# Weight loads of the first two expert rounds wait for a GpSimd write made after the token gather

## The chip, the cores and the metric

The kernel runs on one core of a Trainium2 chip. The metric is the device time of one execution, in microseconds. Its engines are named as the profile names them: PE is TensorE, DVE is VectorE, ACT is ScalarE, POOL is GpSimd, SP is SyncE.

## The reference

A block of masked attention over 8 batches and 8 heads (576 positions, 64 channels a head) feeds a mixture of experts. The output of attention is 4608 tokens of 512 numbers. Routing is done by all pairs of token and expert in order of their score, with a capacity of 576 tokens for each of the 8 experts:

```python
logits = x @ w_gate
order = np.argsort(-logits.flatten())
for idx in order:
    tok, e = (int(idx) // E, int(idx) % E)
    if assigned[tok] >= 0 or counts[e] >= cap:
        continue
    assigned[tok] = e
    counts[e] += 1
for e in range(E):
    mask = assigned == e
    h = np.maximum(x[mask] @ w1[e], 0.0)
    out[mask] = h @ w2[e]
```

All is in float32; w1 is 512x1024 and w2 is 1024x512 for each expert.

## The kernel before, in words

The first third of the time is attention; it writes its result, the tokens x, to a buffer `xd` in device memory. The rest is `moe`, in eight rounds, one for each expert in the order in which experts fill up. Round r finds out which expert is next (`search`), which tokens it takes (`settle`, `listing`), fetches those tokens (`gather`), and runs two products on them (`expert`). The search and the listing of round r+1 lie between the products of round r.

- `gather` fetches 576 tokens by five indirect DMAs that GpSimd issues (four of 128 tokens, one of 64) into `xg`. PE transposes each of them into a PSUM tile (`ptx`, a single buffer from round 1 on; in round 0 `py` too), ACT makes `xh` and DVE makes `xl` from it, so that x = xh + xl in two parts that PE can multiply fast. In round 0 PE also runs filler products on a tile of zeros between the transposes (`keep_clock`).
- `weights` brings one of the 8 tiles of w1 or of w2 (f = 0 to 7, 128x512, 256 KB): SP issues the load into a `raw` buffer (8 for w1, 4 for w2), ACT makes the high part, and the low part comes in one of two ways. Mostly DVE subtracts. For w2 of round 0 and for w1 and w2 of round 1 (`ADDED`), ACT writes the negated high part and GpSimd issues a DMA that adds `raw` to it: an accumulating transfer.
- `expert` runs the first product (`ph`, from `xh`, `xl` and the w1 parts, f = 0 to 7), ACT and DVE bring the result to `hb`, and the second product (`py`, from `hb` and the w2 parts). ACT and DVE bring that to `y`, and GpSimd issues an indirect DMA that scatters it to `out` behind a one-element write (`spacer`).

There are two kinds of DMA queue: SP's loads go through q1, all that GpSimd issues (gathers, scatters, accumulating transfers) through q0. Both run on the same 16 DMA engines.

The order of the instructions on each engine is made by a planner when the program is built (`Schedule`): every step is given an engine, an estimated cost, its dependencies and a boost, and the planner writes the instructions of each engine in the order that its estimates give. The order is fixed; what waits for what on the chip is settled from the buffers that instructions share. A dependency that a step is given in the planner alone moves its place in the order and makes no instruction wait. So it is with `behind` before the change: from tile f = 3 on, the loads of round 0 are planned after the second gather (`got[r, 1]`), and on the chip SP issues them without a wait.

```python
RAW1, D_R, NQ, AHEAD_W = 8, 262, (2, 2), (3,)
def behind(r, f):
    return [got[r, 1]] if r < len(AHEAD_W) and f >= AHEAD_W[r] else []
ld = op("SP", 60, load, [*deps, *old], dma=T_W)
```

Of the kernel before, what the change touches and what calls it, by code (L numbers as in the profile page):

```python
# [36 lines left out]
TOL_DVE, TOL_ACT, TOL_POOL, TOL_PE, T_W = 100, -50, 200, 500, 730  # L37
T_P, T_S, AHEAD = 440, 2150, 5
B_L, B_G, B_T, B_X, B_H, B_HL, B_Y, B_S, B_W = 23000, 27000, 15000, 0, 20000, 17000, 28000, -15000, 1500
RAW1, D_R, NQ, AHEAD_W = 8, 262, (2, 2), (3,)  # L40
ADDED, T_A, T_G = (("2", 0), ("1", 1), ("2", 1)), 4500, 4500
NS, B_E, DIRECT = (2, 2), 3000, 6
B_C = (0, 2500, 20000, 20000, 20000, 20000, 20000, 20000)
# [112 lines left out]
class Schedule:  # L156
# [8 lines left out]
    def op(self, eng, cost, fn, deps=(), boost=0, lat=0, dma=0, buf=None):  # L165
        x = Op(len(self.ops), eng, cost, fn, deps, boost, lat, dma, buf)
        for d in x.deps:
            d.users.append(x)
        self.ops.append(x)
        return x  # L170
# [926 lines left out]
def moe(tc, ctx, C, R, xd, w1, w2, out):  # L1097
    nc = tc.nc
# [4 lines left out]
    NF, ND = FF // 128, DM // 128  # L1103
    CUT = (0, 256, CAP)
    K = Schedule({"DVE": TOL_DVE, "ACT": TOL_ACT, "POOL": TOL_POOL, "PE": TOL_PE})
    op = K.op
# [19 lines left out]

    act = lambda o, i, f=AF.Copy: nc.scalar.activation(o, i, f)  # L1127
    sub = lambda e, o, a, b: e.tensor_tensor(o, a, b, op=OP.subtract)  # L1128
    E, gemm1_end, x_users, got = {}, {}, {}, {}

    def weights(n, r, f, deps):

        raw, old, use = RAW[n].take()

        def load():
            if n == "1":
                src = w1[bass.ds(E[r], 1), f].rearrange("o p d f -> p (o d f)")
            else:
                src = w2[bass.ds(E[r], 1), f * 128:f * 128 + 128, :].rearrange("o p d -> p (o d)")
            nc.sync.dma_start(raw, src)  # L1140

        ld = op("SP", 60, load, [*deps, *old], dma=T_W)
        h, oldh, useh = WH[n].take()
        l, oldl, usel = WL[n].take()
        hi = op("ACT", 525, lambda: act(h, raw), [ld, *oldh], B_W)
        if (n, r) in ADDED:
            use.append(hi)
            ne = op("ACT", 525, lambda: nc.scalar.activation(l, h.bitcast(F32), AF.Copy, scale=-1.0), [hi, *oldl], B_W)
            useh.append(ne)
            lo = op("POOL", 1040, lambda: nc.gpsimd.dma_start(l, raw, accum_op=OP.add), [ne], B_W, lat=T_A)  # L1150
            use.append(lo)
        else:
            lo = op("DVE", 600, lambda: sub(nc.vector, l, raw, h), [ld, hi, *oldl], B_W)
            use += [hi, lo]
        useh.append(lo)
        return h, l, hi, lo, useh, usel


    def chain(eng, cost, fn, deps, boost=None):
        return op(eng, cost, fn, deps, B_C[len(scan)] if boost is None else boost)  # L1160
# [3 lines left out]
    def search(r):  # L1164
        scan.append(r)
        prev = st["next"]
        hold = gemm1_end.get(r - AHEAD)
        g = prev + [hold]
        for v in range(2):
            for it in range(4):  # L1170
                p = chain("PE", T_P, R.counts, g)

                def dve(v=v, it=it):
                    R.step(it, v)
                    if it == 3 and v == 0:
                        R.low()
                        R.flags(R.V2, None, R.kstep(0, True))

                g = [chain("DVE", T_S + (400 if it == 3 and not v else -1050 if it == 3 else 0), dve, [p])]

        def which():
            R.count()
            R.fills()
            R.expert(R.largest())
            R.above()

        return chain("DVE", 2100, which, [g[0], st["fetch"]])

    def settle(r, e):

        if r < NE - 1:
            m = chain("DVE", 1180, R.members, [e], B_L)
            rk = chain("PE", 70, R.ranks, [m], B_L)
            nd = st["need"] = chain("DVE", 310, R.need_of, [m, st.get("slots")], B_L)
        else:
            nd = chain("DVE", 400, R.rest, [e, st["left"], st["slots"]], B_L)
            rk = chain("PE", 70, R.ranks, [nd], B_L)
        ac = chain("DVE", 1000, R.accept, [rk, nd], B_L)
        sl = st["slots"] = chain("DVE", 450, R.slots, [ac, st.get("digits")], B_L)
        ix, box = listing(r, sl)  # L1200
        st["left"] = None
        if r == NE - 2:
            st["left"] = chain("DVE", 200, R.assign, [ac])
        elif r < NE - 1:
            cl = chain("DVE", 1780, R.close, [nd, ix if r == 0 else None])
            lv = chain("DVE", 880, R.leave, [cl, ac])
            oc = chain("ACT", 1055, lambda: R.copies(R.oh, nc.scalar), [lv])
            gf = chain("DVE", 670, R.start, [cl])
            st["next"] = [oc, gf]
        return ix, box  # L1210
# [21 lines left out]
    def gather(r, ix, box):  # L1232

        done = []
        for m, n in enumerate(MSZ):
            xg, old, use = XG.take()

            def get(xg=xg, n=n, m=m):
                nc.gpsimd.indirect_dma_start(out=xg[:n], out_offset=None, in_=xd,  # L1239
                                             in_offset=bass.IndirectOffsetOnAxis(ap=box[0][:n, m:m + 1], axis=0))  # L1240

            g = op("POOL", 1040, get, [ix, *old], B_G, lat=T_G if r else 2600)
            got[r, m] = g
            if r == 0:
                pt, old, usep = (PYR if m % 3 < 2 else PTR).take()
            else:
                pt, old, usep = PTR.take()
            pt = pt.rearrange("p (d x) -> p d x", d=ND)
            a, b = (x[:, :, 128 * m:128 * m + n] for x in (XH, XL))

            def turn(pt=pt, xg=xg, n=n):
                for d in range(ND):
                    nc.tensor.transpose(pt[:, d, :n], xg[:n, 128 * d:128 * d + 128], C["identf"][:n, :n])  # L1253

            t = op("PE", 460 if n == 128 else 250, turn, [g, *old], B_T)
            use.append(t)
            if r == 0:
                turns.append(t)
            full = 500 if n == 128 else 290
            wx = x_users.get((r - 1, 0 if m < 2 else 1), [])  # L1260
            s0 = op("ACT", full, lambda pt=pt, a=a, n=n: act(a, pt[:, :, :n]), [t, *wx], B_T)
            s1 = op("DVE", full + 100, lambda pt=pt, a=a, b=b, n=n: sub(nc.vector, b, pt[:, :, :n], a), [s0], B_T)
            usep += [s0, s1]
            done.append((s0, s1))
        return done
# [6 lines left out]

    def expert(r, X, box, W1, W2):

# [47 lines left out]
        for m, n in sorted(enumerate(MSZ), key=lambda x: x[1] if r == NE - 1 else 0):  # L1322
            py, old, use = PYR.take()
            for f in range(NF):
                hb, _, useb, hl = hidden[f]
                wh, wl, hi, lo, useh, usel = W2[f]

# [39 lines left out]
    def fetch(r, eidx):  # L1367
        E[r] = nc.values_load(eidx[0:1, 0:1], engines=[nc.sync.engine], min_val=0, max_val=NE - 1,
                              skip_runtime_bounds_check_because="the index is the place of a maximum among NE flags")

    X, BOX, W, EN = {}, {}, {}, {}

    def round_(r):
        e = None
        if r:
            e = search(r) if r < NE - 1 else chain("DVE", 650, R.last, [st["fetch"], st["need"]])
        en = st["fetch"] = EN[r] = op("SP", 100, lambda: fetch(r, R.eidx), [e])
        ix, BOX[r] = settle(r, e)
        X[r] = gather(r, ix, BOX[r])
        W[r] = [weights("1", r, f, [en, *behind(r, f)]) for f in range(NF)]  # L1380

    def behind(r, f):

        return [got[r, 1]] if r < len(AHEAD_W) and f >= AHEAD_W[r] else []

    round_(0)
    for r in range(NE):
        W2 = [weights("2", r, f, [EN[r], *behind(r, NF)]) for f in range(NF)]
        expert(r, X[r], BOX[r], W[r], W2)
        if r + 1 < NE:  # L1390
            round_(r + 1)
# [51 lines left out]
def build(tc, T, out):  # L1443
    with ExitStack() as ctx:
        cp = ctx.enter_context(tc.tile_pool(name="const", bufs=1))
        dp = ctx.enter_context(tc.tile_pool(name="scratch", bufs=1, space=DRAM))
        C, load_const = load_consts(tc, cp, T)
        xd = dp.tile([N, DM], F32, name="xd")
        Lt = cp.tile([128, NCH, NE], F32, name="Lt")
        R = Router(tc, ctx, C, Lt)  # L1450
        with ExitStack() as c2:
            attention(tc, c2, C, load_const, T, xd, Lt, R)
        with ExitStack() as c2:
            moe(tc, c2, C, R, xd, T["in_moe_w1"], T["in_moe_w2"], out)
# [15 lines left out]
```

## Time and profile before

| | |
|---|---|
| median of 3 runs | 720.18 us (719.6 to 720.63) |
| profiled execution | 720.37 us |
| its span, first to last instruction | 718.6 us |
| PE busy | 678.6 us, 94% of the span |
| DVE busy | 484.2 us, 67% |
| ACT busy | 291.1 us, 41% |
| POOL busy | 137.3 us, 19% |
| moved by DMA | 104.62 MB |

Times in the rows are microseconds from the start of the span. An instruction's row names what it writes and reads without the buffers' numbers; an idle stretch ahead of it is given with what ended it. Busy time of an engine leaves out register moves, semaphores and SP's DMA issues. The granted clock is a share of PE's full speed: 1.00 is 2.4 GHz, 0.50 is 1.2 GHz. A DMA queue's row gives packets, MB and the share of the 16 engines' time that its packets took in the stretch.

### The profile page before, as it was taken

What the parts mean: (1) busy time and instruction counts of PE and PEld (TensorE: products, weight loads), DVE (VectorE), ACT (ScalarE), POOL (GpSimd) and SP (SyncE); (2) the same over time, 40 slices, a digit from 0 to 9 for tenths busy, and PEclk for the clock granted to TensorE, in tenths of its full rate; (3) what the DMA queues carried; (4) which work ended last, traced back from release to release, by engine and by line L of the source; (5) the groups of instructions that cost most, each with busy time, mean ns of one, the idle gap of its engine ahead of it and who ended that gap; (6) DMA issues with size and microseconds to landing.
All of it is one profiled execution on the core that took longest, in us unless ns stands there. A gap on an engine that the chain in (4) does not pass through costs nothing.

```text
span 718.6 us, 17416 instructions
## 1 busy us (share of the span) xinstructions
PE 678.6 (94%) x6598; PEld 596.5 (83%) x6598; DVE 484.2 (67%) x2081; ACT 291.1 (41%) x617; POOL 137.3 (19%) x204
## 2 busy tenths in 40 slices
PE   7899999999984799799999999999999999999995
PEld 5788889998973598589889879788978978988984
DVE  5578877698237689579679868868978963823300
ACT  3355454543310383575334423514533434423310
POOL 6111111100000332741410310311221031221011
PEclk9999999999975799999999999999999999999998
DMA  9999999972111674978223513511532383122001
GB/s 249 260 269 294 264 301 267 281 198 55 47 35 36 207 147 106 292 172 238 96 67 118 169 63 92 200 45 52 167 135 67 118 291 130 56 74 97 1 22 45
DMA packets 58525, 104.62 MB, mean 146 GB/s; under 512 B 6212, under 2 KB 27844, under 8 KB 58436
## 3 DMA queue, kind: packets, MB, share of 16 engines
q1 hardware_dynamic: 49096, 78.32, 38.0%
q0 software_dynamic: 9344, 25.17, 12.8%
q8 instruction: 52, 0.85, 0.5%
q14 instruction: 33, 0.27, 0.1%
HBM read 78.31 MB, written 18.87 MB: 135 GB/s over the span
## 4 chain that ended last, share of the span: by engine, by line
PE 74%; issue 11%; DVE 6%; DMA 4%; POOL 3%; ACT 1%; POOLq 0%; SPq 0%; DVEq 0%
PE ph L1290 24%; PE py L1332 15%; PE pS L506 9%; PE px L514 6%; PE px L564 3%; PE pS L503 3%; DMA xg<-xd,idx 2%; PE pm L486 2%; PE pz L768 2%; PE ptx L1253 2%; PE px L654 2%; PE py L1335 1%; PE py L1337 1%; POOL out L1358 1%; DMA qs<-in_qd 1%
## 5 line engine op out<-in xcount | busy, mean ns | idle before, releaser
L1332 PE MATMUL py<-w2h,hb 128*128 128x512 f32 x512 | 173.6, 403 | 1.4 <-ACT w2h L1127 1.3
L1290 PE MATMUL ph<-xh,w1h 128*128 128x256 f32 (+1 forms) x512 | 138.7, 301 | 0.0
L1290 PE MATMUL ph<-xl,w1h 128*128 128x256 f32 (+1 forms) x512 | 136.2, 297 | 0.0
L1290 PE MATMUL ph<-xh,w1l 128*128 128x256 f32 (+1 forms) x512 | 136.0, 296 | 0.0
L1332 PEld LDWEIGHTS py<-w2h,hb 128*128 128x128 f32 x512 | 97.3, 190 | 21.8 <-ACT w2h L1127 2.3
L1332 PE MATMUL py<-w2l,hb 128*128 128x512 f32 x256 | 101.3, 396 | 0.8 <-DVE w2l L1128 0.5
L1127 ACT ACTIVATE hb<-ph 128x256 fp32r<-128x256 f32 (+2 forms) x192 | 59.7, 346 | 103.1 <-PE ph L1290 102.3
L1290 PEld LDWEIGHTS ph<-xh,w1h 128*128 128x128 f32 x512 | 91.5, 190 | 0.4
L1290 PEld LDWEIGHTS ph<-xh,w1l 128*128 128x128 f32 x512 | 91.6, 190 | 0.0
L1290 PEld LDWEIGHTS ph<-xl,w1h 128*128 128x128 f32 x512 | 91.5, 190 | 0.0
L506 PE MATMUL pS<-q,k 128*80 128x96 f32 (+1 forms) x672 | 84.2, 267 | 0.0
L1358 POOL DMA_INDIRECT out<-y,idx x40 | 40.1, 1003 | 205.9 <-ACT y L1127 145.0
L456 ACT ACTIVATE E<-pS 96x384 f32<-96x384 f32 (+1 forms) x96 | 46.7, 486 | 71.5 <-PE pS L506 70.4
L1310 DVE SCALAR_TENSOR_TENSOR hb<-ph,hb 128x320 fp32r<-128x320 f32 (+1 forms) x128 | 57.4, 453 | 26.5 <-ACT hb L1127 22.5
L506 PEld LDWEIGHTS pS<-q,k 128*80 128x80 f32 (+1 forms) x672 | 69.7, 161 | 0.1
L1127 ACT ACTIVATE y<-py 128x512 f32<-128x512 f32 (+1 forms) x40 | 23.9, 596 | 104.9 <-PE py L1332 90.1
L493 DVE CUSTOM_DVE_ANT_0 junkm<-pm,const 128x80 bf16<-128x80 f32 (+1 forms) x336 | 59.4, 243 | 5.1 <-PE pm L486 4.5
L1332 PEld LDWEIGHTS py<-w2l,hb 128*128 128x128 f32 x256 | 48.8, 191 | 10.6 <-DVE w2l L1128 1.1
L514 PE MATMUL px<-v,E 81*64 81x65 f32 (+1 forms) x1344 | 47.7, 225 | 2.9 <-ACT E L456 2.4
L1127 ACT ACTIVATE w1h<-raw 128x512 fp32r<-128x512 f32 x64 | 38.5, 628 | 29.3 <-DVE oa L1060 22.0
L1239 POOL DMA_INDIRECT xg<-xd,idx x40 | 40.2, 1005 | 50.1 <-PE ph L1290 31.1
L1128 DVE TENSOR_TENSOR w2l<-raw,w2h 128x512 fp32r<-128x512 f32 x48 | 31.7, 685 | 26.4 <-ACT w2h L1127 22.9
(168 smaller groups left out, 1036.5 us busy)
## 6 DMA issues: line engine op xcount, KB each, us to landing
raw<-in_moe_w SPq DMA_DIRECT2D x128, 256.0 KB, 3.7
v<-in_vp SPq DMA_DIRECT2D x8, 780.0 KB
v<-in_vd SPq DMA_DIRECT2D x8, 650.0 KB
xd<-xs SPq DMA_DIRECT2D x16, 288.0 KB, 8.9
xd<-xs SPq DMA_DIRECT2D x32, 144.0 KB, 10.0
w2l<-raw POOLq DMA_DIRECT2D x16, 256.0 KB
qs<-in_qp SPq DMA_DIRECT2D x7, 576.0 KB, 8.6
k<-in_kp SPq DMA_DIRECT2D x7, 576.0 KB, 10.4
```

What stands on the lines that cost most here:

```text
L456: e = self.op("ACT", 380, lambda j=j, pS=pS: nc.scalar.activation(self.E[:self.nk, j * self.gs:j * self.gs + self.gs], pS.tile[:, :self.gs ...
L493: nc.vector.tensor_tensor_reduce(out=jk[:, c - c0, :nk], in0=pm[:, (c - c0) * nk:(c - c0 + 1) * nk], in1=mm[:, min(1, (c if self.kind == 0 ...
L503: nc.tensor.matmul(pS[:nk, c - c0], ls[:64 + n, c], self.r[:64 + n, :2 * nq], start=(c == c0), stop=False, skip_group_check=True)
L506: nc.tensor.matmul(pS[:nk, c - c0], self.Ks[c], self.Qm[c], start=False, stop=True, skip_group_check=True)
L514: nc.tensor.matmul(px[64 * a:64 * a + 64, c - c0], lh, self.V[c][a], start=True, stop=True)
L1127: act = lambda o, i, f=AF.Copy: nc.scalar.activation(o, i, f)
L1128: sub = lambda e, o, a, b: e.tensor_tensor(o, a, b, op=OP.subtract)
L1239: nc.gpsimd.indirect_dma_start(out=xg[:n], out_offset=None, in_=xd, in_offset=bass.IndirectOffsetOnAxis(ap=box[0][:n, m:m + 1], axis=0))
L1290: nc.tensor.matmul(o, a[:, d * 128:d * 128 + 128], b[:, d, c0:c1], start=((d, i) == pairs[0]), stop=((d, i) == pairs[-1]))
L1310: hl = op("DVE", 335 if j == 0 else 400, lambda: nc.vector.scalar_tensor_tensor(hb[:, CAP + c0:CAP + c1], o, 0.0, hb[:, c0:c1], op0=OP.max ...
L1332: nc.tensor.matmul(py, x, w, start=(f + i == 0), stop=(f == NF - 1 and i == 2))
L1358: s = nc.gpsimd.indirect_dma_start(out=out, out_offset=bass.IndirectOffsetOnAxis(ap=box[0][:n, m:m + 1], axis=0), in_=y[:n], in_offset=None)
```

## The change

`behind` goes. In its place, when the tile f = `AHEAD_W[r]` of w1 of round r is planned, GpSimd gets a step that writes one zero into the `raw` buffer of that tile, planned after the second gather and after the last users of the buffer. The load writes the same buffer, so on the chip it waits for the write. The steps of all later tiles of that round, of w1 and w2, depend on it in the planner, and on SP they stand behind the waiting load. `AHEAD_W` goes from (3,) to (3, 4): in round 0 three tiles of w1 are loaded ahead of the write, in round 1 four.

```diff
-RAW1, D_R, NQ, AHEAD_W = 8, 262, (2, 2), (3,)
+RAW1, D_R, NQ, AHEAD_W = 8, 262, (2, 2), (3, 4)
...
-    E, gemm1_end, x_users, got = {}, {}, {}, {}
+    E, gemm1_end, x_users, got, gate = {}, {}, {}, {}, {}
 
     def weights(n, r, f, deps):
 
         raw, old, use = RAW[n].take()
+        if n == "1" and r < len(AHEAD_W) and f == AHEAD_W[r]:
+
+            gate[r] = op("POOL", 100, lambda: nc.gpsimd.memset(raw[:1, :1], 0.0), [got[r, 1], *old], B_G)
+        if r in gate:
+            deps = [*deps, gate[r]]
...
-        W[r] = [weights("1", r, f, [en, *behind(r, f)]) for f in range(NF)]
-
-    def behind(r, f):
-
-        return [got[r, 1]] if r < len(AHEAD_W) and f >= AHEAD_W[r] else []
+        W[r] = [weights("1", r, f, [en]) for f in range(NF)]
...
-        W2 = [weights("2", r, f, [EN[r], *behind(r, NF)]) for f in range(NF)]
+        W2 = [weights("2", r, f, [EN[r]]) for f in range(NF)]
```

The order of PE, of DVE and of SP is the same in both programs, row for row. What moves stands on GpSimd and ACT, and SP gets two waits.

SP, the loads of round 0, now (`raw10` to `raw17` are the buffers of w1, `raw20` to `raw23` those of w2; the rows between are register moves):

```order
L1145 DMA raw11_3213<-in_moe_w1 128x512
L1145 ISA
L1145 DMA raw12_3214<-in_moe_w1 128x512
L1145 ISA
L1145 DMA raw13_3215<-in_moe_w1 128x512 [waits Pool_49]
L1145 ISA
L1145 DMA raw14_3216<-in_moe_w1 128x512
L1145 ISA
L1145 DMA raw20_3220<-in_moe_w2 128x512
```

The fourth load, of `raw13`, now waits for GpSimd, and the rest stand behind it; before, none of these rows had a wait for GpSimd. In round 1 the fifth, of `raw14`, has it. On GpSimd in round 0 the write stands right behind the fifth gather.

GpSimd at the gathers of round 1, before:

```order
L1239 DMA xg4_3260<-xd_66,idx_4375 64x512
L1150 DMA w1l3_3243<-raw13_3215 128x512
L1150 DMA w1l4_3244<-raw14_3216 128x512
L1150 DMA w1l5_3245<-raw15_3217 128x512
L1150 DMA w1l6_3246<-raw16_3218 128x512
L1150 DMA w1l7_3247<-raw17_3219 128x512
L1357 MEMSET spacer_3204 1x1
L1358 DMA out_0<-y2_3274,idx_3642 4608x512
```

and now:

```order
L1244 DMA xg4_3260<-xd_66,idx_4367 64x512
L1155 DMA w1l3_3243<-raw13_3215 128x512
L1136 MEMSET raw14_3216 1x1
L1362 MEMSET spacer_3204 1x1
L1363 DMA out_0<-y2_3274,idx_3642 4608x512
L1362 MEMSET spacer_3204 1x1
L1363 DMA out_0<-y0_3272,idx_3642 4608x512
L1155 DMA w1l4_3244<-raw14_3216 128x512
L1155 DMA w1l5_3245<-raw15_3217 128x512
```

The write stands behind the five gathers and the accumulating transfer of tile 3; those of tiles 4 to 7 move behind two scatters and later.

ACT around the x copies of round 1, before:

```order
L1127 ACTIVATE w1h4_3228<-raw14_3216 128x512
L1148 ACTIVATE w1l4_3244<-w1h4_3228 128x512
L1127 ACTIVATE w1h5_3229<-raw15_3217 128x512
L892 ACTIVATE ohr_4399<-oh_4388 128x1152
L1148 ACTIVATE w1l5_3245<-w1h5_3229 128x512
L1127 ACTIVATE w1h6_3230<-raw16_3218 128x512
L1148 ACTIVATE w1l6_3246<-w1h6_3230 128x512
L1127 ACTIVATE y2_3274<-py0_3209 128x512
L1127 ACTIVATE w1h7_3231<-raw17_3219 128x512
L1148 ACTIVATE w1l7_3247<-w1h7_3231 128x512
L1127 ACTIVATE xh_3261<-ptx0_3211 128x4x128 x2
L1127 ACTIVATE y0_3272<-py1_3210 128x512
```

and now:

```order
L892 ACTIVATE ohr_4389<-oh_4379 128x1152
L1127 ACTIVATE y2_3274<-py0_3209 128x512
L1127 ACTIVATE xh_3261<-ptx0_3211 128x4x128 x2
L1127 ACTIVATE w1h4_3228<-raw14_3216 128x512
L1127 ACTIVATE y0_3272<-py1_3210 128x512
L1127 ACTIVATE xh_3261<-ptx0_3211 128x4x128
L1153 ACTIVATE w1l4_3244<-w1h4_3228 128x512
L1127 ACTIVATE w1h5_3229<-raw15_3217 128x512
L1153 ACTIVATE w1l5_3245<-w1h5_3229 128x512
L1127 ACTIVATE w2h0_3232<-raw20_3220 128x512
L1153 ACTIVATE w2l0_3248<-w2h0_3232 128x512
L1127 ACTIVATE xh_3261<-ptx0_3211 128x4x128
```

Tiles 4 to 7 of w1 move behind the first two x copies, and tile 4 now stands ahead of the copy of `y0` and of the third x copy.

## Rows read from the trace of the kernel before

**Rows 1.** The page: busy us (share of the span) xinstructions.

```profile
PE 678.6 (94%) x6598; PEld 596.5 (83%) x6598; DVE 484.2 (67%) x2081; ACT 291.1 (41%) x617; POOL 137.3 (19%) x204
```

**Rows 2.** PE's waits in 228:246, 246:410, 315:719: us, times, longest.

```profile
PE py L1253 <- DMA xg<-xd,idx: 2.8, 1, 2.8
...
PE ptx L1253 <- DMA xg<-xd,idx: 4.3, 1, 4.3
...
PE py L1332 <- ACT w2h L1127: 1.3, 1, 1.3
```

**Rows 3.** GpSimd's timeline: start, us, instruction, idle time before.

```profile
237.85 1.45 POOL L1239 DMA_INDIRECT xg<-xd,idx  x1 [3.35 <-DVE idx L1092]
...
243.38 0.91 POOL L1239 DMA_INDIRECT xg<-xd,idx  x1 [0.30 <-issue]
254.10 0.99 POOL L1150 DMA_DIRECT2D w2l<-raw  x1 [9.81 <-ACT w2l L1148]
...
285.93 0.87 POOL L1150 DMA_DIRECT2D w1l<-raw  x1
...
288.56 0.85 POOL L1150 DMA_DIRECT2D w1l<-raw  x1 [0.33 <-ACT w1l L1148]
...
291.06 1.03 POOL L1239 DMA_INDIRECT xg<-xd,idx  x1 [0.30 <-DVE A L1039]
...
297.43 0.97 POOL L1150 DMA_DIRECT2D w1l<-raw  x1 [0.34 <-issue]
...
304.60 0.09 POOL L1357 MEMSET spacer<- 1x1 f32 x1
...
342.58 1.08 POOL L1239 DMA_INDIRECT xg<-xd,idx  x1 [7.13 <-issue]
```

**Rows 4.** SP's timeline, 230:236.4: first start, us from first to last end.

```profile
230.19 6.27 SPq L1140 DMA_DIRECT2D raw<-in_moe_w  x12
```

**Rows 5.** DMA queues in 239:240 and in 240:241: packets, MB, share.

```profile
q1 hardware_dynamic: 208, 0.39, 100.3%
...
q0 software_dynamic: 24, 0.10, 24.6%
```

**Rows 6.** The chain in 220:360, round 0: start, us, what.

```profile
237.85 5.78 DMA xg<-xd,idx
...
249.30 3.98 PE ph L1290 x28
```

**Rows 7.** Stretches: us, busy (x) of each engine, PEclk, DMA share, GB/s.

```profile
243.25:243.50 0.25, 0.00 (x0) 0.00 (x0) 0.00 (x0) 0.00 (x0) 0.12 (x1) 0.50 0.65 229
302.00:304.00 2.00, 2.00 (x7) 1.62 (x6) 1.57 (x7) 0.26 (x1) 1.55 (x4) 0.50 1.11 209
```

**Rows 8.** DMA queues in 290:296.5.

```profile
q0 software_dynamic: 425, 0.81, 65.8%
q1 hardware_dynamic: 522, 0.95, 43.4%
```

**Rows 9.** The same chain, round 1.

```profile
291.06 9.71 DMA xg<-xd,idx
...
302.07 2.70 PE py L1332 x6
...
305.21 2.07 PE py L1332 x9
```

**Rows 10.** DMA queues in 344:345.5 (round 2).

```profile
q0 software_dynamic: 73, 0.25, 57.2%
```

**Rows 11.** DMA queues in 255.5:258.5 (two accumulating transfers of round 0).

```profile
q0 software_dynamic: 267, 0.51, 100.7%
```

**Rows 12.** A stretch with one search step on DVE (columns as in rows 7).

```profile
302.90:305.35 2.45, 2.45 (x11) 1.92 (x10) 2.21 (x11) 0.11 (x1) 1.51 (x4) 0.65 1.12 201
```

**Rows 13.** The tile raw in 225:345; and the page's DMA issues (last: median us).

```profile
DMA to landing us min/median/max: 3.0/4.9/5.5
...
raw<-in_moe_w SPq DMA_DIRECT2D x128, 256.0 KB, 3.7
```

## The prediction, made before the changed kernel ran

> **What bounds the kernel now.** I read the page first, then TensorE's waits, the timelines of GpSimd and SyncE, the DMA queues stretch by stretch, the chain of waits and the granted clock. TensorE is busy for 678.6 us, 94% of the span [rows 1]. The reader is to see that it sets the end: from 315 us on its longest wait is 1.3 us, so whatever an earlier stage gives or loses arrives at the end unchanged. Two of its waits are for the token gather: 2.8 us in expert round 0 and 4.25 us in round 1 [rows 2]. In these two rounds the change holds weight loads back.
>
> Round 0: GpSimd issues the five gathers from 237.85 to 244.29 [rows 3]. SyncE has by then posted twelve weight loads of 256 KB, from 230.19 on [rows 4]. In the microsecond from 239 they hold all of the DMA engines (100.3%); the gathers' queue q0 gets 24.6% in the next [rows 5]. The first transposes start 5.8 us after the first issue, and the dense products at 249.30 [rows 6]. In that wait the granted clock falls to 0.50, the lower of its two levels (1.2 GHz) [rows 7].
>
> Round 1: in GpSimd's order [rows 3] and so on q0 the gathers stand behind three accumulating transfers and a scatter. From 290 to 296.5 q0 moves 0.81 MB, about the three (0.79 MB), while the weight loads on q1 move 0.95 MB beside them [rows 8]. The first transposes come 9.71 us after the first issue [rows 9], and again the clock is at 0.50 afterwards [rows 7].
>
> **The change part by part.** PE, DVE and SP keep their order; GpSimd gets two one-element writes, and ACT and GpSimd take four weight tiles of round 1 later. The writes themselves cost nothing: the spacer write of the same size takes 0.09 us, and after the gathers of round 0 GpSimd has no work until 254.10 [rows 3]. What counts is what they hold: the gated load and everything behind it on SP, where only weight loads stand.
>
> *Round 0.* Three loads (0.79 MB) go out at once and are through by about 235; the other nine go out from about 244.6, when the gathers have been issued. So the gathers have the engines to themselves. The nearest row is round 2, where no weight load runs: the first gather, issued from 342.58 [rows 3], moves 0.25 MB between 344 and 345.5 [rows 10], and is through 2.9 us after its issue began. Here the first issue takes 0.37 us longer (1.45 against 1.08), so the data would be through at 241.1; landing needs a little more. Ends: 241.1 (2.6 us gained) and 243.67 (nothing). I take 241.9, near the uncontended row: **1.8 us**. At the lower clock transposes and filler take about 1.5 us a gather, slower than the 1.25 us between GpSimd's issues, so the whole chain up to 249.30 moves by that; at the full clock it would gain some 0.4 more. The late weights are covered: nine tiles, 2.36 MB, at the 0.39 MB a microsecond of the hardware queue alone [rows 5] are in by about 252, the first of them near 248.3, and its product is wanted some 9 us behind the first dense one, at about 256.
>
> *Round 1.* Four loads (1.05 MB) go out ahead of the gate and are through by about 287. The three accumulating transfers, issued from 285.93 on and the last from 288.56 [rows 3], then run alone. Two such transfers moved 0.51 MB in the 3 us from 255.5 [rows 11], 1.5 us each: they would be through at 291.7 instead of 296.5, the scatter at 292.6, the first gather, whose issue ends at 292.10, at about 294, landed by 295. TensorE wants it at 296.56. So the wait of 4.25 us goes, and with it the fallen clock: after the wait six products take 2.70 us, a moment later nine take 2.07 [rows 9]; 1.32 us lost there and 0.53 on transposes and counts, 1.85 in all. What is late next is the single buffer of the transposes. ScalarE and VectorE must empty it, VectorE in turn with a search step of 2.45 us [rows 12]; counted through, the third, fourth and fifth transposes would wait 0.3, 0.2 and 0.35 us, of which 0.15 is there already: 0.7 to be taken off. **4.25 + 1.85 - 0.7 = 5.4 us**. Ends: 0 (the transfers in front stay as slow) and 6.1.
>
> The price of the gate there: the write stands behind the fourth accumulating transfer, issued from 297.43 [rows 3], so the fifth load goes out at about 298.8. Loads take 3.0 to 5.5 us to land in this stretch, 3.7 in the median of all [rows 13]: 301.8 to 304.3, I take 302.5. ScalarE now has that tile ahead of a y copy and of the third x copy, which it would finish at 304.2; VectorE, after its search step, can start on that copy at 304.1. So it is just hidden; at 304.3 it would cost 1.8 us. The last w2 tile would be ready near 328 and is wanted after 335.
>
> **One rule against it.** The Trainium skill (DMA: Bandwidth & Descriptors, section Queues, rings and completion order) says that each DMA engine takes turns between the queues that have work, a packet at a time. By that rule the first gather of round 0 has its half of the engines already, and the sum there would be 0.7 us instead of 1.8. The rows from 239 to 241 do not agree with it [rows 5]; those from 290 to 296.5, with 65.8% and 43.4%, come near it [rows 8].
>
> **The sum.** 1.8 + 5.4 = 7.2 us off the profiled execution's 720.37 is 713.2. The median of the runs shown is 0.2 below that execution, so **713.0**.
>
> **Rivals.** (1) *Even turns.* In round 0 the gather has its share already and waits mostly for something fixed; emptying q1 saves half of the 1.4 us that its data takes alone, 0.7: 720.2 - 0.7 - 5.4, about 714.1. For it: both queues move in round 1. Against it: q0 has a quarter of the engines in the microsecond from 240, two issues on. (2) *The accumulating transfers are the brake by themselves.* They keep most of their 6.5 us without q1, the first gather lands near 299.5, and round 1 gives 1.3 us with the low clock still there: 720.2 - 1.8 - 1.3, about 717.0. Against it: 1.5 us each [rows 11]. (3) *Slower: ScalarE stands, in order, before the fifth tile of round 1.* From 302.5 on each microsecond that this tile lands later keeps the y copy, the third x copy and then TensorE waiting by as much. It decides from 309.7 on (302.5 + 7.2), 10.9 us after the issue; at 313 the time would be 723.5. Against it: no landing in this stretch took over 5.5 us [rows 13]. (4) *The hold holds nothing*, the loads being through before it acts or the gathers not bound by them: 720.2. Against it: twelve loads are posted before the first gather [rows 3, 4].
>
> **How the numbers follow.** Forecast 0.67, (1) 0.14, (2) 0.11, (4) 0.04, (3) 0.04. About 0.2% (1.4 us) is what can be told from no change here. Forecast, (1) and (2) are faster by more, less a hundredth for weak mixtures: 0.91; within 0.2%: 0.05; slower: 0.04. The low end takes both upper ends (2.6 + 6.1 = 8.7 us, 711.5) and half a microsecond of spread between runs: 711.0. The high end takes in (1), (2), and a fifth tile that costs its 1.8 us: 717.0.
>
> **What would show it.** Right: TensorE's two waits for the gather shrink, to about 1 us near 241 and to none near 296; q1 is empty from about 235 to 245 and from 287 to 299; no stretch at clock 0.50 around 300; the first transposes of round 1 start some 5.5 us after the gather's first issue instead of 9.71. Wrong: ScalarE's wait for the gated tile of round 1 is over 2 us and TensorE waits for x copies; or q0 still takes over 2 us for each accumulating transfer with q1 empty; or in round 0 the dense products start as long after the gather's first issue as before.

## The result, and the profile after

The changed kernel took 717.01 us in the median of 18 runs (713.69 to 722.36 but for one run that was disturbed), the kernel before 720.44 beside it. The ratio is 0.9939 with a 95% interval of 0.9916 to 0.9962: 4.4 us faster, between 2.7 and 6.1. On the 720.18 us shown before, that is 715.8; forecast were 713.0 and a range of 711.0 to 717.0. The profiled execution took 714.34 us, its span 712.6 (before 720.37 and 718.6).

The page of the changed kernel, busy us by engine:

```profile
PE 675.7 (95%) x6596; PEld 594.9 (83%) x6598; DVE 483.9 (68%) x2081; ACT 290.9 (41%) x617; POOL 138.5 (19%) x206
```

PE works 2.9 us less than before [rows 1], though its instructions are the same: it spends less time at the low clock. Its waits show the rest. The changed kernel, PE's waits in 228:246 and in 246:400 (us, times, longest), to be held against [rows 2]:

```profile
PE py L1258 <- DMA xg<-xd,idx: 2.0, 2, 1.4
...
PE ptx L1258 <- DMA xg<-xd,idx: 0.8, 1, 0.8
...
PE ptx L1258 <- DVE xl L1128: 1.7, 1, 1.7
```

The two waits for the gather, 2.8 and 4.25 us in one piece each, have become three of at most 1.4 us in round 0, whose sum is still 2.8, and none in round 1. In round 1 stands a new one of 1.7 us, for `xl`. Now what the hold did. GpSimd's timeline of the changed kernel (start, us, idle time before), beside [rows 3]:

```profile
238.02 1.46 POOL L1244 DMA_INDIRECT xg<-xd,idx  x1 [3.35 <-DVE idx L1092]
...
243.56 0.91 POOL L1244 DMA_INDIRECT xg<-xd,idx  x1 [0.30 <-issue]
244.47 0.09 POOL L1136 MEMSET raw<- 1x1 f32 x1
...
289.85 1.03 POOL L1244 DMA_INDIRECT xg<-xd,idx  x1 [0.30 <-DVE A L1039]
...
295.87 1.00 POOL L1155 DMA_DIRECT2D w1l<-raw  x1
296.48 0.43 POOL L1136 MEMSET raw<- 1x1 f32 x1
```

SP's timeline, the first load behind each write (first start, us from first to last end, loads in the stretch):

```profile
244.58 1.57 SPq L1145 DMA_DIRECT2D raw<-in_moe_w  x3
...
296.94 2.37 SPq L1145 DMA_DIRECT2D raw<-in_moe_w  x4
```

The loads go out 0.1 and 0.5 us after the writes start. Until then q0 has the DMA engines to itself; the same kernel's queues in 235:244 and in 287:290, where before q1 held all engines [rows 5] or 43.4% of them [rows 8]:

```profile
q0 software_dynamic: 235, 0.79, 28.2%
...
q0 software_dynamic: 278, 0.50, 98.9%
```

In the second stretch q0 moves 0.50 MB in 3 us, about two accumulating transfers at 1.5 us each, as they took alone before [rows 11]. The chain of the changed kernel in 236:325, beside [rows 6, 9]:

```profile
243.56 3.92 DMA xg<-xd,idx
...
247.99 3.97 PE ph L1295 x28
...
299.21 0.66 PE ptx L1258 x4
...
309.62 3.98 PE ph L1295 x28
```

It gives the three distances by which everything below is judged, since whole runs of one kernel scatter by 3 to 5 us to either side: **R0**, from the first gather's issue in round 0 to the first dense product, 11.45 us before and 9.97 now; **R1**, from there to round 1's, 65.54 before and 61.63 now; the rest, 403.8 and 403.0. So in the one profile round 0 gave 1.5 us and round 1 gave 3.9. The clock, same kernel (columns as in [rows 7], where both stretches stand at 0.50):

```profile
243.25:243.50 0.25, 0.16 (x1) 0.17 (x2) 0.22 (x1) 0.00 (x0) 0.01 (x1) 1.00 0.88 295
302.00:304.00 2.00, 2.00 (x18) 1.59 (x15) 1.63 (x9) 1.75 (x4) 0.97 (x1) 1.00 1.05 404
```

And the new wait, first as PE's timeline has it, then ACT's, both of the changed kernel:

```profile
295.12 0.60 PE L1258 MATMUL ptx<-const,xg 128*128 128x128 f32 x4
...
299.21 0.66 PE L1258 MATMUL ptx<-const,xg 128*128 128x128 f32 x4 [1.74 <-DVE xl L1128]
```

```profile
297.83 0.60 ACT L1127 ACTIVATE xh<-ptx 128x512 fp32r<-128x512 f32 x1 [3.96 <-remote]
...
301.14 0.63 ACT L1127 ACTIVATE w1h<-raw 128x512 fp32r<-128x512 f32 x1 [0.64 <-DMA raw<-in_moe_w]
```

Round 1's first transposes come 5.27 us after the first issue (9.75 before) and end at 295.72. ScalarE has been idle since 293.87, yet its copy begins 2.1 us later, at 297.83, and the view names no releaser ("remote"). The trace has one semaphore for which this copy waits, that of PE. It rises at 297.81, and PE's next signal, for products recorded up to 296.00, comes at 298.64. So ScalarE waits for nothing but PE's signal; whether PE finished later than its records say or only signalled late, they don't tell. The second transposes need the same buffer and wait. The gated tile itself is harmless: ScalarE waits 0.64 us for it.

### The profile page after: what moved, and what is told of

The parts are those of the page before. It is cut to its first block, busy times and chain, and to the rows that moved or that the text cites. A ratio compares the mean times of both kernels' runs of the same rounds, so it can differ in the third digit from the quotient of the medians.

```text
span 712.6 us, 17418 instructions
## 1 busy us (share of the span) xinstructions
PE 675.7 (95%) x6596; PEld 594.9 (83%) x6598; DVE 483.9 (68%) x2081; ACT 290.9 (41%) x617; POOL 138.5 (19%) x206
## 4 chain that ended last, share of the span: by engine, by line
PE 71%; issue 12%; DVE 7%; DMA 4%; POOL 4%; ACT 1%; another core or an unknown queue 1%; SPq 0%; POOLq 0%; DVEq 0%
PE ph L1295 22%; PE py L1337 14%; PE pS L506 9%; PE px L514 6%; PE px L564 3%; PE pS L503 3%; DMA raw<-in_moe_w 2%; PE pm L486 2%; PE pz L768 2%; PE px L654 2%; PE ptx L1258 2%; PE py L1340 1%; PE py L1342 1%; POOL out L1363 1%; DMA qs<-in_qd 1%
## 5 line engine op out<-in xcount | busy, mean ns | idle before, releaser
L1337 PE MATMUL py<-w2h,hb 128*128 128x512 f32 x512 | 171.4, 399 | 1.2 <-ACT w2h L1127 1.2
L1127 ACT ACTIVATE y<-py 128x512 f32<-128x512 f32 (+1 forms) x40 | 23.9, 596 | 102.5 <-PE py L1337 89.3
L514 PEld LDWEIGHTS px<-v,E 81*64 81x64 f32 (+1 forms) x1344 | 42.4, 138 | 7.1 <-ACT E L456 1.9
```

Of the source, the lines that this page charges most:

```text
L514: nc.tensor.matmul(px[64 * a:64 * a + 64, c - c0], lh, self.V[c][a], start=True, stop=True)
L1337: nc.tensor.matmul(py, x, w, start=(f + i == 0), stop=(f == NF - 1 and i == 2))
```

## The experiments

Twelve kernels, each in five rounds beside the kernel before. "First T" is the time from a round's first gather issue to its first transposes, "copy" from round 1's first issue to its first copy of x; R0 and R1 as above, all from each run's one profile. The ratio has its 95% interval.

| kernel | R0 first T | R0 | R1 first T | copy | R1 | ratio to before |
|---|---|---|---|---|---|---|
| before | 5.82 | 11.45 | 9.75 | 10.62 | 65.54 | |
| changed | 3.88 | 9.97 | 5.27 | 7.98 | 61.63 | 0.9939 (0.9916 to 0.9962) |
| e1 hold in round 0 only | 3.95 | 11.51 | 9.21 | 10.36 | 67.82 | 0.9978 (0.9949 to 1.0006) |
| e2 hold in round 1 only | 5.57 | 10.10 | 5.37 | 7.23 | 61.10 | 0.9953 (0.9923 to 0.9983) |
| e3 order, no hold | 5.63 | 11.45 | 9.46 | 10.61 | 66.21 | 1.0024 (0.9991 to 1.0057) |
| e4 changed again | 3.89 | 10.09 | 5.19 | 7.97 | 61.66 | 0.9958 (0.9924 to 0.9992) |
| e5 until landed | 3.89 | 9.74 | 5.38 | 8.00 | 62.69 | 0.9943 (0.9911 to 0.9976) |
| e6 two buffers | 3.91 | 9.91 | 5.08 | 5.91 | 60.85 | 0.9995 (0.9962 to 1.0029) |
| e7 e5 and e6 | 3.88 | 9.84 | 5.10 | 5.91 | 62.42 | 1.0000 (0.9973 to 1.0028) |
| e8 two more free | 3.86 | 9.92 | 5.20 | 8.77 | 63.98 | 0.9963 (0.9935 to 0.9992) |
| e9 round 1 from fourth | 3.87 | 10.25 | 5.32 | 5.95 | 59.72 | 0.9953 (0.9922 to 0.9984) |
| e10 round 1 from third | 3.92 | 9.94 | 5.34 | 5.97 | 59.92 | 0.9935 (0.9900 to 0.9969) |
| e11 e10 and e5 | 3.88 | 9.74 | 5.33 | 5.96 | 60.67 | 0.9956 (0.9924 to 0.9988) |
| e12 e10's order, no hold | 3.88 | 10.08 | 7.35 | 8.04 | 61.64 | 0.9953 (0.9924 to 0.9982) |

**Which part acts: e1 to e4.** In e1 to e3 a write that is to hold nothing goes into a tile of its own, here e3:

```diff
-    spacer = pw.tile([1, 1], F32, name="spacer")
+    spacer, free = (pw.tile([1, 1], F32, name=x) for x in ("spacer", "free"))
...
-lambda: nc.gpsimd.memset(raw[:1, :1], 0.0)
+lambda: nc.gpsimd.memset(free, 0.0)
```

For e1 the target is `free if r else raw[:1, :1]`, for e2 `raw[:1, :1] if r else free`; e4 is the changed kernel.

> The order of every engine is that of the changed kernel; only round 1's write goes into a tile of its own, so that round 1's loads are held by nothing, and round 0's are held. Theory A (the hold itself pays, by keeping the weight loads off the DMA engines while the gather lands): round 0 as in the changed kernel, 10.0 us from the first gather's issue to the first product of the first layer (11.45 in the kernel before); round 1's first transposes again 9.5 to 10 us after the first gather's issue, with a PE wait of some 4 us. Time 1.5 us under the kernel before (ratio 0.998). Theory B (in round 1 the order that came with it pays: the copies of x ahead of the splits of tiles 4 to 7): round 1's first transposes within 6 us of the issue without the hold, ratio 0.994.

> The same order, but round 0's write goes into a tile of its own: only round 1's loads are held. Theory A: round 0 as before the change, 11.4 us from the first issue to the first product of the first layer, first transposes 5.8 us after the issue; round 1 as in the changed kernel, first transposes some 5.3 us after the issue, no PE wait for the gather near 296. Time 3.9 to 4.7 us under the kernel before (ratio 0.994). Theory B: the same time. If round 0's hold did nothing (a rival of the prediction), the time is that of the changed kernel and round 0 still reads 10.0 us.

> Both writes go into a tile of their own: the order of the changed kernel without any hold. Theory A: both rounds as before the change (11.4 us in round 0, first transposes of round 1 9.5 to 10 us after the issue), ratio 1.000, between 0.998 and 1.002. Theory B: round 1's gain of 3.9 us stays, ratio 0.994 to 0.996.

> The changed kernel unchanged, a second time. In its first profile the first copy of x in round 1 began 2.1 us after its transposes had ended, and the next transposes waited 1.74 us for it. Theory C (the lateness comes with this order of work and this load on the DMA engines): it stands again at the same place with 1.5 to 2.2 us. Theory D (it is chance of one execution): it is away, round 1 is 1.5 us shorter (60.1 instead of 61.6 us from the first product of round 0's first layer to that of round 1), or it stands elsewhere. Ratio 0.994 in either case.

Round 1 came out as theory A had it: with the hold (e2, e4) R1 is 61.1 and 61.7, without it (e1, e3) 67.8 and 66.2 (in e1 1.5 us of it are a fallen clock, below), and order alone gains nothing. The kernel e3, PE's waits in 297:325, and its chain:

```profile
PE ptx L1258 <- DMA xg<-xd,idx: 4.0, 1, 4.0
```

```profile
244.97 5.58 DMA xg<-xd,idx
...
256.42 3.98 PE ph L1295 x28
...
298.22 9.41 DMA xg<-xd,idx
```

Round 0 did not. The hold brings its first transposes forward by 1.6 to 2.0 us every time, but its end only sometimes: without the hold e2 ends at 10.10, as good as with it and as its expectation has it for a hold that does nothing, and with the hold e1 ends at 11.51. The chains of e2 and then of e1 say why:

```profile
238.72 5.52 DMA xg<-xd,idx
...
248.82 3.98 PE ph L1295 x28
```

```profile
246.47 5.46 DMA xg<-xd,idx
...
252.43 5.49 PE ph L1295 x28
```

In e2 the first gather is late, but at full clock PE makes the time good by the fifth. In e1, and in the changed kernel, the chain goes instead through the fifth gather, the last that GpSimd issues (3.92 us in the changed kernel, 5.46 in e1). What made R0 11.45 in the kernel before and in e3 is the clock, which fell inside the round: in the kernel before at 243.18, within a stand of PE of 2.85 us, in e3 0.9 us behind one of 2.04 us. The kernel e3, a stretch with the granted clock (columns as in [rows 7]):

```profile
251.75:254.75 3.00, 3.00 (x15) 2.71 (x14) 2.03 (x3) 2.07 (x4) 0.00 (x0) 0.50 0.28 97
```

In e2 PE stood for 1.68 us and the clock did not fall; in the eleven profiles with round 0 held it fell in none before the fifth transposes. But in e1 it fell 0.5 us behind them, after a stand of 1.64 us for the late fifth gather, and the next 28 products took 5.49 us instead of 3.98; the table has that under R1. So in round 0 the hold is worth 0.1 us where the clock stays up, less than the held profiles differ among themselves, and 1.4 where it would have fallen: two of three profiles without the hold and one of eleven with it, too few for a rate. In time a gain by round 0's hold is not shown: the interval of e1 takes in 1, and e2's overlaps that of the changed kernel.

The late copy of round 1 stood in e4 at the same place, 2.2 us behind its transposes' end, and PE waited 1.80 us for it (theory C).

**The end of round 0, and the one buffer: e5 to e7.** In e5 the write waits until the fifth gather has landed:

```diff
-lambda: nc.gpsimd.memset(raw[:1, :1], 0.0)
+lambda: nc.gpsimd.memset(raw[:1, :1], 0.0) if r else nc.gpsimd.tensor_copy(raw[:1, :1], XG.tiles[4][:1, :1])
```

In e6, in `gather`:

```diff
-                pt, old, usep = PTR.take()
+                pt, old, usep = (PHR[0] if r == 1 and m % 2 else PTR).take()
```

> The changed kernel, but round 0's write into the fourth tile copies one element of the fifth gather's buffer, so that it waits until that gather has landed and not only until it is issued; the order on every engine is the same. In three profiles with the hold of round 0 the fifth gather took 3.9, 4.1 and 5.5 us from issue to use and ended the wait for round 0, since the released loads start 0.1 us after the write and run beside its last packets. Theory E (round 0 ends with the fifth gather's landing, and the loads released at its issue delay it): 3.3 to 3.6 us from its issue to its transposes, first issue to the end of round 0's fifth transposes 9.3 to 9.6 us (9.97, 10.10 and 11.50 held until the issue; 11.45, 11.45 and 10.10 not held). Theory F (GpSimd's issues, one in 1.25 us, set the end and the loads cost nothing): 9.9 to 10.1 us as in two of the three. Theory G (the loads now come too late): ACT waits more than 1 us for a tile of w1 and the first layer stalls. Ratio 0.994 to 0.995 in E and F, 0.996 or more in G.

> The changed kernel, but in round 1 the second and fourth transposes write to a buffer of the first layer's products, so that the second transposes don't wait for the copies of the first to leave the one buffer (the rest of PE's order is the same; GpSimd issues the gather ahead of one scatter and behind one accumulating transfer). Theory A (the part of round 1's gain that is missing is the wait for the one buffer, 1.74 us in the first profile of the changed kernel): no PE wait for xl at the second transposes, round 0's end to round 1's 59.9 to 60.3 us instead of 61.6. Theory H (the first copy's lateness is a delay that every later step takes over): the wait moves to the third transposes, and the distance stays 61.1 to 61.7.

> Both edits together: the hold of round 0 until the fifth gather has landed, and two buffers for round 1's transposes. If theories E and A both hold, first issue of round 0 to the end of round 1's transposes is 9.5 + 60.1 = 69.6 us (71.6 and 71.75 in the two profiles of the changed kernel, 76.99 before), and the ratio to the kernel before 0.990; if neither, 71.6 us and 0.994.

The kernel e5, GpSimd's timeline, and its chain at the fifth gather:

```profile
249.84 0.18 POOL L1136 COPY raw<-xg 1x1 f32<-1x1 f32 x1 [2.78 <-DMA xg<-xd,idx]
```

```profile
246.15 3.63 DMA xg<-xd,idx
```

From its issue, the fifth gather takes 3.63, 3.27 and 3.44 us on the chain where loads wait for its landing (e5, e7, e11) and 3.85 to 5.46 in the seven kernels that release them at its issue and have it on the chain. R0 is 9.74 to 9.84 against 9.91 to 11.51. So theory E held in its cause, though not in its 9.3 to 9.6 us: the loads released at the issue do slow the last gather, by about half a microsecond, and once by two. The Trainium skill (DMA: Bandwidth & Descriptors, section Queues, rings and completion order) says that an engine's semaphore write lands only behind its earlier writes of all queues. The trace does not show that as the cause here: it is the data packets of the gathers that end later, the last of them 8.70 to 9.10 us after round 0's first issue in six of the seven kernels and 10.22 in e1, against 8.38 to 8.73 in the three; from the last 4-byte packet on q0, a semaphore's, to the last landing it takes 0.37 to 0.69 us in the seven and 0.45 to 0.59 in the three.

But theory G held too, and it costs more than E gives. The kernel e5, ACT's timeline, and PE's waits in 236:330:

```profile
252.69 0.63 ACT L1127 ACTIVATE w1h<-raw 128x512 fp32r<-128x512 f32 x1 [1.55 <-DMA raw<-in_moe_w]
```

```profile
PE pz L768 <- DVE G L782: 0.8, 1, 0.8
```

ScalarE waits 1.55 us for a late tile, VectorE then for ScalarE, and PE stands 0.8 us in the first layer for a step of VectorE. R1 is 62.69 against 61.63 and 61.66 (the changed kernel and e4), and in the other two pairs 62.42 against 60.85 (e7, e6) and 60.67 against 59.92 (e11, e10). So the hold until landing gains 0.1 to 0.35 us in R0 and loses 0.7 to 1.6 in R1, in each of the three pairs. In whole runs neither is seen: e5's ratio of 0.9943 is not the 0.996 or more of theory G.

e6 told less than it was meant to. PE's order did not stay as its expectation says: the planner put round 1's transposes towards the end of round 0's second layer, and its gather 4.5 us later after round 0's first dense product. R1 fell to 60.85, the copy came promptly, and the wait moved to the fifth transposes. PE's timeline of e6:

```profile
311.25 0.69 PE L1258 MATMUL ptx<-const,xg 64*128 64x64 f32 x4 [2.87 <-DVE xl L1128]
```

Both kernels with that edit lose it all later: from round 1's dense products to the end they take 410.0 and 410.2 us, the other twelve 400.6 to 406.7. A part is a stand of PE for the next search, 2.3 us at 337.5 in e6 and 2.1 at 336.0 in e7, with the clock at 0.50 for 3.4 us behind it; the rest is not explained. e7, which was to need 69.6 us from round 0's first issue to round 1's dense products if theories E and A held and 71.6 if neither did, needs 72.3. The two leave theory A of the one buffer undecided.

**How much must be held, and what makes the copy late: e8 to e12.** In e8 the write goes two tiles further, in e9 and e10 round 1's hold begins earlier:

```diff
-lambda: nc.gpsimd.memset(raw[:1, :1], 0.0)
+lambda: nc.gpsimd.memset(RAW["1"].tiles[f + 2][:1, :1], 0.0)
```

```diff
-RAW1, D_R, NQ, AHEAD_W = 8, 262, (2, 2), (3, 4)
+RAW1, D_R, NQ, AHEAD_W = 8, 262, (2, 2), (3, 3)
```

with (3, 2) in e10. e11 is e10 with e5's copy; e12 is e10 with round 1's write into `free`.

> The changed kernel, but the writes go into the tiles two further on: round 0's loads go free up to the fifth tile, round 1's up to the sixth, and only those behind are held; every engine's order is the same. Theory A (what pays is an empty load queue while the gather runs, so loads that have landed by then may go free): round 0's first transposes 3.9 to 4.4 us after the first issue, round 1's 5.2 to 5.4 us after it without a wait of PE for the gather, ratio as the changed kernel, 0.994 to 0.996. Theory I (each held load counts by itself): half of the gain goes, round 0's first transposes at 4.9, round 1's at 7.5 us, ratio 0.997.

> The changed kernel, but round 1's loads are held from the fourth tile on instead of the fifth (PE, DVE, ACT and SP keep their order; on GpSimd the accumulating transfer of the fourth tile goes behind the gather and two scatters). It is to tell why the first copy of x in round 1 comes some 2 us after its transposes (7.2 to 8.8 us after the first gather's issue in five profiles, the later the more transfers were on their way). Theory J (the transfers beside the gather make it late): the copy begins 7.0 to 7.5 us after the first issue, PE's wait for xl at the second transposes is 1.0 us or less, round 0's end to round 1's 60.5 to 61.2. Theory K (it belongs to the place in PE's stream): 7.9 to 8.0 us, wait 1.7, 61.6. Rival L (the tile is late now): ACT waits over 2 us for raw and the second half of the transposes with it, 63 us or more.

> The same with round 1's loads held from the third tile on; on GpSimd the accumulating transfers of the third and fourth tiles go behind the gather, so that only the first two of them can run beside it. Theory J: the copy begins 6.0 to 7.0 us after the first issue, PE's wait for xl 0.5 us or less, 59.9 to 60.5 from round 0's end to round 1's. Theory K: 7.9 to 8.0 us, wait 1.7, 61.6. Rival L: ACT waits over 2 us for raw, the first layer starts late or stalls, 63 us or more and a ratio of 0.998 or more.

> Round 1's loads held from the third tile on, as in the run that showed no late copy, and round 0's until the fifth gather has landed instead of issued. Theory E: first issue to the end of round 0's fifth transposes 9.7 to 9.9 us (9.74 and 9.84 in the two profiles with this hold) and no profile above 10; round 1 as in that run, 59.7 to 60.0 us, without a wait of PE for xl. Ratio to the kernel before 0.993, and within 0.2% of that run, since the two differ by 0.1 to 0.3 us where the fifth gather isn't disturbed.

> The order of the kernel that holds round 1 from the third tile on (the accumulating transfers of its third and fourth tiles behind the gather), round 0 held as in the change, but round 1's write in a tile of its own, so that round 1's weight loads run free beside the gather. Theory M (the weight loads are the brake): round 1's first transposes again 9.0 to 9.8 us after the first issue, PE waits 3.5 us or more for the gather, round 0's end to round 1's 65 to 68 us, ratio 0.998 to 1.002. Rival N (the accumulating transfers are the brake, 0.5 MB in 3 us beside the gather in the kernel before): first transposes at 5.3 us, 60 us, ratio 0.993. Between them: each has its share, 7 to 8 us and 62 to 64.

e8: both first transposes are as early as with the full hold, as theory A says, but the copy of round 1 is later still, and R1 2.3 us longer (part of it a clock that fell to 0.50 at 304.3). ACT's timeline of e8:

```profile
302.64 0.60 ACT L1127 ACTIVATE xh<-ptx 128x512 fp32r<-128x512 f32 x1 [4.82 <-remote]
```

e9 and e10 took the lateness away altogether, e9 more than theory J forecast: the copy begins 0.63 us after its transposes do, R1 is 59.72 and 59.92, and PE does not stand for ScalarE's wait for the held tile, 1.69 and 1.87 us. (ACT's order was not the same after all: the splits of the newly held tiles moved behind two copies of x.) ACT's timeline and the chain of e10:

```profile
296.10 0.60 ACT L1127 ACTIVATE xh<-ptx 128x512 fp32r<-128x512 f32 x1 [1.88 <-PE ptx L1258]
298.30 0.60 ACT L1127 ACTIVATE xh<-ptx 128x512 fp32r<-128x512 f32 x1 [1.60 <-PE ptx L1258]
300.77 0.63 ACT L1127 ACTIVATE w1h<-raw 128x512 fp32r<-128x512 f32 x1 [1.87 <-DMA raw<-in_moe_w]
```

```profile
243.59 3.89 DMA xg<-xd,idx
...
247.99 3.97 PE ph L1295 x28
...
307.45 0.46 PE ptx L1258 x4
```

But theory J is not shown by that. In e9 q0 moves as much around the gather as in the changed kernel (0.89 MB in the six microseconds before the first issue and 0.85 in the four behind it, 0.91 and 0.85 there), and three accumulating transfers still stand ahead. What moved is the fourth tile, its load, its splits on ScalarE and its accumulating transfer at once.

e12 shows that the brake of round 1 has two parts. With the loads free but only two accumulating transfers ahead of the gather, the first transposes come at 7.35 us, between 9.46 (three ahead, e3) and 5.34 (two and the hold, e10). Its chain, and PE's waits for the gather by `ptx` in both rounds, the longest in round 1:

```profile
293.81 7.30 DMA xg<-xd,idx
```

```profile
PE ptx L1258 <- DMA xg<-xd,idx: 2.5, 2, 1.9
```

So neither theory M nor rival N alone: moving the third accumulating transfer behind the gather (in e3 the fourth is there already; here it moves further back, and ScalarE's splits of both move with them) gives 2.1 us, the hold another 2.0 and more, where PE's own work then ends the wait.

e11 has R1 60.67, outside its forecast of 59.7 to 60.0: PE stands 0.7 us in the first layer as in e5. As times, e9 to e12 can't be told from the changed kernel, since all the intervals overlap; e10 has the lowest ratio, and in the stretch from round 0's first issue to round 1's dense products e9 to e11 need 70.0, 69.9 and 70.4 us against 71.6 and 71.8 of the changed kernel. But the lead does not last: some 18 us later PE stands 2.0, 1.5 and 2.0 us for VectorE's step of the next search, against 0.2 and 0.9 in the two profiles of the changed kernel. From round 0's first issue to the end of that stand it is 88.6, 88.0 and 89.0 us against 88.3 and 89.3. The kernel e10, PE's waits in 236:330:

```profile
PE pz L1014 <- DVE ge L977: 1.5, 1, 1.5
```

## Why the prediction was right, and where it was off

**Direction and mechanism** were right for round 1: a hold on the load queue frees the engines for the gather, and that alone pays (e2 against e3, which differ in nothing else). In round 0 the mechanism was not the one forecast. The two rounds gave 5.4 us together where 7.2 were forecast.

**Round 1, forecast 5.4, measured 3.9.** Two of its three terms held: PE's wait of 4.25 us went, and the low clock with it. The step that was mis-sized is the third, 0.7 to be taken off where 4.25 + 1.85 - 3.9 = 2.2 were: "counted through, the third, fourth and fifth transposes would wait 0.3, 0.2 and 0.35 us". It let the first copy follow its transposes at once. The runs showed a copy 2.1 us late, and a wait of 1.74 us at the second transposes, which was not in the count; of the three that were counted the waits show 0.14 us at the fifth. Where the copy is prompt (e9, e10), round 1 gives 5.8 and 5.6 us: the forecast size. The fifth tile was forecast to go out 7.7 us after the first issue and to be there at 11.4; it went at 7.1 and was there at 11.3.

**Round 0, forecast 1.8, measured 1.5**, but not for the reason given: that the two are near is luck. The first transposes came 3.88 us after the first issue (forecast 4.05); the failed step is "the whole chain up to 249.30 moves by that". It does not: the fifth gather, issued 5.5 us after the first, sets the end at about 9.9 us whatever the first one does (e2). The 1.5 us are the fallen clock that did not come.

**The rule** of the Trainium skill that was weighed against it (DMA: Bandwidth & Descriptors, section Queues, rings and completion order) would have made the sum 0.7. The rows from 239 to 241 that the prediction sets against it [rows 5] cannot test it: q0's first packet comes at 240.24, 2.39 us after the first issue, and with q1 empty none comes before 2.16 us either. The trace also records when each of a transfer's sixteen parts lands. Those of that gather land 3.32 to 3.83 us after the issue in the changed kernel. In the kernel before, fourteen are in by 4.32, each about half a microsecond later, the next at 4.76 and the last at 5.78; in e3 the lateness is spread over more of them, up to 5.58. So most parts in the kernel before lost less than the 0.7 of the rule, and PE's wait ends with the last part. That the loads cause the 1.6 to 2.0 us is shown; that they do it by taking the engines' time, as the forecast has it, is not, and what keeps the last part no row says. At the round's end the loads cost 0.1 us at full clock (e2), for another reason, the fifth gather.

**The rivals.** Even turns (1) by their price, and a hold that holds nothing (4), are out for the first transposes by the rows above; for the end of round 0, (4) is what e2 shows where the clock stays up. The accumulating transfers (2) are not the brake by themselves, 1.5 us each when alone, but with one fewer of them ahead of the gather half of its delay beside the loads is gone (e12), which neither the forecast nor the rival had. ScalarE before the fifth tile (3) waited 0.64 us. Of the signs named for right, all but one stood: PE's wait near 241 fell only to 1.4, with two more behind it. Of those named for wrong, PE's wait for an x copy came, without ScalarE's wait for the tile.

**Left open:** why the first copy is late. It grew with two more loads free (e8) and went when the fourth tile was held (e9); through what, no row says. Transfers beside the gather are not enough by themselves: in e12 all loads run there and the copy follows 0.69 us behind the start of its transposes. The trace has the transposes finished, ScalarE idle and PE's signal late. In the five kernels with the late copy it also has only 2 to 7 of the sixteen landings of each gather of round 1, so when these were complete is not known there.

## What to carry to other kernels

Where a gather meets bulk loads, hold the loads by a true dependency; a few tiles loaded ahead cover the gap. Then price the release as well: held until the gather had landed instead of issued, the late loads cost more behind the gather than it gained. Count what else stands on the gather's own queue: here one transfer fewer ahead went with half of the delay. Before a gain at the first of several arrivals is booked, look which arrival the stage's end hangs on. And follow a gain to the next wait behind it: that of e9 to e11 was gone at the next search.

## What the hardware showed unexpectedly

- The first gather took 3.86 to 3.95 us from its issue to its first use in eleven profiles with an empty load queue, 5.57 to 5.82 in the three with full ones.
- The copy that follows the first transposes can begin 1.9 to 3.6 us after they start although the recorded work of PE is over after 0.6 (R1: e2, changed, e4, e5, e8); PE's records then run on at full pace.
- The part ahead of the first gather, the same instructions in all fourteen kernels, ended between 237.85 and 245.92 us. That is over half of the 15 us between the shortest and the longest of their spans.
- The clock fell with stands of PE of 2.85 and 2.04 us, and in e1 of 1.64, but not with one of 1.68 in e2: the length of the stand alone does not tell it.
- Of the sixteen parts of one gather beside loads, fifteen landed by 4.76 us after the issue and the last at 5.78 (kernel before, round 0).
